# A spectral mixer on one core: the second forward product with real and imaginary halves in one 512-column operand, the row exchange on ScalarE, and a new table of ranks

## The chip, the cores and the metric

The kernel runs on one core of one Trainium2 chip, as one program. The metric is the device time of one execution in microseconds (us), the median of three runs. A core has five engines that work side by side, each through its own queue in order: TensorE (PE, matrix products, with a row of its own, PEld, for the loads of the weights), VectorE (DVE), ScalarE (ACT), GpSimd (POOL, which here issues transfers that add in memory) and SyncE (SP, which issues the other transfers). Matrix products are written to PSUM; other operands lie in SBUF, over 128 partitions.

## The reference

Two branches work on the same input x (2048 rows, 512 columns) and are mixed by a gate per row:

```python
def reference(A_x, A_w_r, A_w_i, B_x, B_w1, B_b1, B_w2, B_b2, gate_w):
    g = sigmoid((x * gate_w).sum(-1, keepdims=True))
    X = rfft2(x, axes=(-2, -1)) * (w_r + 1j * w_i)      # x = A_x
    a = irfft2(X, s=(S, D), axes=(-2, -1))
    b = einsum("bsf,fd->bsd", gelu(einsum("bsd,df->bsf", x, w1) + b1), w2) + b2
    return g * a + (1 - g) * b                           # S, D, F = 2048, 512, 1792
```

Everything is float32. The kernel splits each operand of a product into a high part of 12 bits and a low rest (names ending in h and l), and adds three products: high with high, high with low, low with high.

## The kernel before

**The transform branch.** The 2048 rows are taken as 16 blocks j of 128 rows (row 16a + j of x is row a of block j). `forward(j)` folds a block's 512 columns on VectorE into even and odd parts (tiles `eo`, then `cl`, also shown under the name of the buffer `xr` it reuses), splits them (`eoh`, `eol`) and multiplies by the cosine and sine table `cf` on PE: for c = 0 (real) and c = 1 (imaginary) a product into PSUM tile `pd`, four matmuls of 260 columns and four of 130 per block. ScalarE and VectorE cut `pd` into `x..h` and `x..l`. Then comes the second forward product, a transform over the 128 rows of the block: `py`, with the table `tf` of cosines (64 columns) and sines (64 columns) as weights. Real and imaginary parts need the two halves of `tf` in opposite order, so ScalarE first widens `tf` from 128 to 192 columns (line 710), and each c has three matmuls of 258 columns into a PSUM tile of its own: two high ones (`s_high`) and a low one (`s_low`), six per block. ScalarE copies `py0` to `pys` (line 757), VectorE adds it to `py1` for the real half of `y` (line 758) and subtracts it for the imaginary half, whose two sets of 64 rows change places: on VectorE itself for the first four blocks (line 767), and with a subtraction on VectorE (line 761) and two copies on ScalarE (line 764) for the other twelve. Radix-4 steps over the blocks (`stage1`), the multiplication by the spectral weights (`filt`) and the way back (`stage4`, `inverse`: products `pz` and `pa`) follow.

**The dense branch.** `mlp(half, c)` runs for two halves of F and four groups c of 512 rows: products `ph` (w1; 12 matmuls of 512 columns for each of 7 blocks of F), gelu on ScalarE (line 1106), a split into `g..h` and `g..l`, and products `po` (w2). Partial results go to memory and are added there by POOL's transfers.

**What sets the order.** Each operation is a step of a graph with a cost and an engine; a planner (`Graph.schedule`) plays the engines through and takes, whenever one is free, the ready step of lowest rank whose buffers can be had. The ranks stand in a table of numbers, `RANKS`, one for each step, which replaces the ranks in the code. So the order of every engine's queue, SP's transfers included, comes out of `RANKS`, of the costs (`c_vec`, `c_act`, `c_pe`) and of the numbers of buffers (`slots`, `most`); on the chip each queue then runs in that order, and an operation that waits holds up what stands behind it on its engine. A helper `mm` issues every matmul, so all of PE's rows show one line, 530.

The start: eleven matmuls on zeros warm PE up; then the first `ph` is made in two halves, for two row blocks each (blocks 0 and 4, then 8 and 12), from `mxh` (ScalarE, line 649) and `mxl` (VectorE, line 650), the high part and the rest of x. The end: the last `pa` goes through ScalarE (`od`, line 999) and VectorE (`uv`, `y`, `o`), while PE makes the last `po` in half-width products.

Of the kernel before, what the change touches and what calls it, by code (L numbers as in the profile page):

```python
# [11 lines left out]
F32 = mybir.dt.float32  # L12
# [5 lines left out]
P = 128  # L18
# [154 lines left out]
class Graph:  # L173
# [282 lines left out]
def tile_kernel(ctx: ExitStack, tc: tile.TileContext, xt, w1, w2, b1, b2, x0g, wf, wrev, out, consts):  # L456
# [13 lines left out]
             "so": 2, "ba": 2,  "pf": 2, "pm": 4, "ti": TI, "ring": RING, "hw": 8}  # L470

    whole = ("xr", "xm", "wra", "wrb", "e2", "z", "ttab", "xhl", "wa", "wb", "hid", "so", "ba", "ctab", "gb")
    most = {("pm", "ph"): 2, ("pm", "po"): 2, ("pm", "po0"): 1, ("pm", "py"): 3, ("t2k", "pq"): 2}
    g = Graph(slots, most)
    add = g.add

# [17 lines left out]
    def c_pe(n, k=1):  # L494
        return k * (n / 2400 + 0.0135) + 0.005
# [795 lines left out]
```

## Time and profile before

| what | value |
|---|---|
| median of 3 runs | 372.75 us (372.29 to 372.97) |
| span of the profiled execution, first to last instruction | 370.8 us, granted PE clock 0.999 |
| what the median has beyond the span | 1.95 us |
| PE busy | 365.1 us, 1838 matmuls |
| VectorE busy | 327.5 us, 691 instructions |
| ScalarE busy | 229.6 us, 454 instructions |
| POOL busy | 44.1 us |
| mean transfer rate | 170 GB/s, 62.99 MB |

The page gives no time of its own for the profiled execution beside its span. "Busy" counts time in which an instruction of the engine was under way. PE's matmuls overlap each other, so the time that one adds is read from the step between two starts and not from its own duration. "Idle before" and the bracket behind a row name the time an engine stood still ahead of an instruction and what ended it; a name with q at the end (SPq) is the engine's issuing part. The chain of waits is followed back from the last instruction.

### The profile page before, as it was taken

To read this page: it belongs to the slowest core of one execution; us is meant where nothing else is said; L and a number is where in the kernel's file an instruction comes from. 1 tells how busy PE (TensorE), PEld (TensorE's weight loads), DVE (VectorE), ACT (ScalarE), POOL (GpSimd) and SP (SyncE) were. 2 spreads that over 40 slices of the span, in tenths; PEclk is the share of its full clock that TensorE was granted. 3 is DMA by queue.
4 is the path that set the end of the run, shared out by engine and by line. 5 is a ranking of instruction groups with operands and counts; after the bars stand their busy time and mean duration, and the time that the engine had idled before them with its cause. 6 is when DMAs were issued, how large, how long until landed. Compare 5 with 4: busy or idle time off the path is not lost.

```text
span 370.8 us, 5565 instructions
## 1 busy us (share of the span) xinstructions
PE 365.1 (98%) x1838; PEld 309.9 (84%) x1838; DVE 327.5 (88%) x691; ACT 229.6 (62%) x454; POOL 44.1 (12%) x54
## 2 busy tenths in 40 slices
PE   8999999999999999999999999999999999999995
PEld 6888888888888888888888888888888888888885
DVE  4999999999999789999999999588849696789996
ACT  5776587976678735375367213894697549457830
POOL 0000000000000002021032020001403222221031
PEclk9999999999999999999999999999999999999999
DMA  8962899425954216479289762318968999736268
GB/s 276 389 194 73 257 282 342 147 71 151 289 173 141 77 23 170 142 157 256 72 214 267 225 120 55 57 25 291 209 130 112 211 285 187 130 88 139 88 85 198
DMA packets 50868, 62.99 MB, mean 170 GB/s; under 512 B 4656, under 2 KB 31344, under 8 KB 50064
## 3 DMA queue, kind: packets, MB, share of 16 engines
q1 hardware_dynamic: 43496, 49.54, 41.3%
q0 software_dynamic: 7200, 12.85, 23.1%
q8 instruction: 14, 0.23, 0.2%
q10 hardware_dynamic: 144, 0.26, 0.2%
q14 instruction: 14, 0.11, 0.1%
HBM read 38.64 MB, written 23.73 MB: 168 GB/s over the span
## 4 chain that ended last, share of the span: by engine, by line
PE 95%; DVE 1%; DMA 1%; issue 0%; ACT 0%; SPq 0%; DVEq 0%
PE ph L530 41%; PE po L530 40%; PE pz L530 4%; PE pd L530 4%; PE py L530 3%; PE pa L530 3%; DMA xr<-in_xt 1%; DVE uv L1002 0%; DVE y L1021 0%; SPq L588 0%; DVE y L1024 0%; DVE mxl L650 0%; DVE o L1168 0%; ACT mxh L649 0%; ACT od L999 0%
## 5 line engine op out<-in xcount | busy, mean ns | idle before, releaser
L1106 ACT ACTIVATE ph<-ph,b1t 128x512 f32<-128x512 f32 x56 | 36.9, 659 | 41.5 <-PE ph L530 39.9
L949 ACT ACTIVATE sw<-y,al 64x512 f32<-64x512 f32 x32 | 23.0, 722 | 2.2 <-DVE y L812 1.6
L908 DVE TENSOR_TENSOR m<-y,wf 128x514 f32<-128x514 f32 x32 | 20.8, 689 | 0.2
L956 DVE SCALAR_TENSOR_TENSOR pq<-y,al,sw 128x256 f32<-128x256 f32 x32 | 14.4, 481 | 5.9 <-ACT sw L952 5.5
L521 POOL DMA_DIRECT2D bacc<-o x12 | 10.5, 877 | 73.2 <-ACT o L1155 60.2
L521 POOL DMA_DIRECT2D wa7l<-in_w x1 | 1.0, 1017 | 141.0 <-ACT wa7l L582 141.0
L1155 ACT ACTIVATE o<-po 128x512 f32<-128x512 f32 x12 | 7.1, 595 | 15.9 <-PE po L530 15.8
L1152 ACT ACTIVATE o<-po,b2t 128x512 f32<-128x512 f32 x16 | 10.7, 686 | 7.6 <-PE po L530 7.5
L1002 DVE TENSOR_TENSOR uv<-pa,od 128x512 f32<-128x512 f32 x16 | 10.6, 685 | 3.6 <-ACT od L999 3.5
L764 ACT ACTIVATE y<-pys 64x257 f32<-64x257 f32 x24 | 10.0, 418 | 5.2 <-DVE pys L761 4.8
L530 PE MATMUL pd<-cf,eoh 128*128 128x260 f32 x64 | 12.7, 285 | 0.0
L688 DVE TENSOR_TENSOR eo<-xr 128x256 f32<-128x256 f32 x30 | 12.0, 418 | 0.0
L530 PEld LDWEIGHTS pd<-cf,eoh 128*128 128x128 f32 x64 | 10.6, 189 | 1.5 <-issue 0.2
L999 ACT ACTIVATE od<-pa 128x512 f32<-128x512 f32 x8 | 4.8, 599 | 10.2 <-PE pa L530 9.9
L952 ACT ACTIVATE sw<-y 1x512 f32<-1x512 f32 x16 | 10.1, 629 | 0.4
L530 PE MATMUL pd<-cf,eol 128*128 128x130 f32 x64 | 10.3, 253 | 0.0
L702 DVE TENSOR_TENSOR xr<-eo 128x256 f32<-128x256 f32 x24 | 9.8, 418 | 0.1
L530 PEld LDWEIGHTS pd<-cf,eol 128*128 128x128 f32 x64 | 9.6, 189 | 0.1
L649 ACT ACTIVATE mxh<-xm 128x512 fp32r<-128x512 f32 x12 | 6.9, 623 | 3.7 <-PE ph L530 3.7
L650 DVE TENSOR_TENSOR mxl<-xm,mxh 128x512 fp32r<-128x512 f32 x12 | 7.8, 686 | 1.2 <-ACT mxh L649 1.2
L705 DVE TENSOR_TENSOR eol<-xr,eoh 128x512 fp32r<-128x512 f32 x12 | 8.3, 688 | 0.2
L1046 DVE SCALAR_TENSOR_TENSOR ba<-gb,ba 128x512 f32<-128x512 f32 x12 | 8.1, 685 | 0.3 <-DMA ba<-bacc 0.3
(713 smaller groups left out, 1353.6 us busy)
## 6 DMA issues: line engine op xcount, KB each, us to landing
wf<-in_wf SPq DMA_DIRECT2D x16, 257.0 KB, 4.9
bacc<-o SPq DMA_DIRECT2D x16, 256.0 KB, 3.3
xr<-in_xt SPq DMA_DIRECT2D x15, 256.0 KB, 3.5
war<-in_w SPq DMA_DIRECT2D x14, 256.0 KB, 3.5
wbr<-in_w SPq DMA_DIRECT2D x14, 256.0 KB, 3.5
xm<-in_xt SPq DMA_DIRECT2D x12, 256.0 KB, 4.3
bacc<-o POOLq DMA_DIRECT2D x12, 256.0 KB, 4.0
ba<-bacc SPq DMA_DIRECT2D x12, 256.0 KB, 3.2
```

The lines of the kernel that those rows point to most:

```text
L521: return add("pool", kb / 150, 3.4, lambda: nc.gpsimd.dma_start(dst(), src(), accum_op=ALU.add), reads, writes, rank)
L530: pe.matmul(ps, w, x, start=start, stop=stop)
L688: v(lambda s=s, op=op: vec.tensor_tensor(eo.ap()[:, s], x.ap()[:, 0:2], x.ap()[:, 2:4], op=op), 256, [x], [(eo, s)], FEED)
L702: v(lambda k=k, op=op: vec.tensor_tensor(quarter(cl, k), eo.ap()[:, :, 0], eo.ap()[:, :, 1], op=op), 256, [eo], [(cl, k)] if j % 4 == 0 or ...
L764: a(lambda o=o, i=i: act.activation(Y[j].ap()[o:o + HP, 1], pys.ap()[i:i + HP, 1], AF.Copy), 257, [(pys, 1)], [(Y[j], 1 + k)], 0, more=0.1)
L908: v(lambda mk=mk, k=k, y=y, w=w: vec.tensor_tensor(mk.ap(), y.ap(), w.ap()[:, k:k + 1, :ND].to_broadcast([P, 2, ND]), op=ALU.mult), 514, [ ...
L949: a(lambda sw=sw, y=y, o=o, i=i: act.activation(sw.ap()[o:o + HP], y.ap()[i:i + HP, ::-1, :HD], AF.Copy, scale=al.ap()[i:i + HP, 0:1]), 51 ...
L952: a(lambda sw=sw, y=y, j=j: act.activation(sw.ap()[HP:HP + 1], y.ap()[HP:HP + 1, ::-1, :HD], AF.Copy, scale=math.cos(math.pi * j / NJ)), 5 ...
L956: v(lambda sw=sw, pq_=pq_, y=y, j=j, k=k, op=op: vec.scalar_tensor_tensor(pq_.ap()[:, k], y.ap()[:, k, :HD], al.ap()[:, 1 + j:2 + j], sw.a ...
L1002: v(lambda i=i, op=op: vec.tensor_tensor(uv.ap()[:, :, i], ps.ap()[:, 0], od.ap(), op=op), 512, [ps, od], [(uv, i)], 2)
L1106: a(lambda f=f, ps=ps: act.activation(ps.ap(), ps.ap(), AF.Gelu_apprx_tanh, bias=b1t.ap()[:, f:f + 1]), 600, [b1t], [ps], 0.9 if half else ...
L1152: a(lambda o=o, ps=ps, q=q: act.activation(o.ap(), ps.ap(), AF.Identity, scale=-1.0, bias=b2t.ap()[:, q:q + 1]), 600, [b2t, ps], [o])
```

## The change

In `forward(j)` the cut of `pd` keeps 128 columns from each of its two parts instead of 129, so that `x..h` and `x..l` hold the real and the imaginary half side by side in 2 x 256 = 512 columns. The second forward product then has `tf` as it is loaded (128 columns, not widened) as weights and all 512 columns as moving operand: two high matmuls and one low one per block, into one PSUM tile `py`. The imaginary half comes out with its two sets of 64 rows in the wrong places; ScalarE exchanges them in two copies of 64 rows out of PSUM into one of two buffers `sh` (used in turn, with a column of zeros in the middle, written once by two small memsets). VectorE's addition and subtraction then read `py` and `sh`, over 256 columns; the last of the 257 columns of `y` is made by two one-column copies on ScalarE.

```diff
-    most = {..., ("pm", "py"): 3, ...}
+    most = {..., ("pm", "py"): 2, ...}
     def c_pe(n, k=1):
-        return k * (n / 2400 + 0.0135) + 0.005
+        return k * max(n / 2400 + 0.0135, 0.112)
...
+    sh = [one(f"sh{k}", [P, ND], parts=3) for k in range(2)]
+    for b in sh:
+        add("vec", 0.1, 0.1, lambda b=b: vec.memset(b.ap()[:, P:P + 1], 0.0), [], [(b, 2)], 0.7)
...
-        t = buf("ttab", [P, 2, P + HP], F32R, f"tf{j}", parts=2)
-        dma(lambda: raw(t.ap()[:, :, :P], tf_d[j]), 128, [], [(t, 0)])
-        a(lambda: act.activation(t.ap()[:, :, P:], t.ap()[:, :, :HP], AF.Copy), P, [(t, 0)], [(t, 1)])
+        t = buf("ttab", [P, 2, P], F32R, f"tf{j}")
+        dma(lambda: raw(t.ap(), tf_d[j]), 128, [], [t])
...
-            return some(c, [[511, 2], [1, P + 1]], 1 + k * NC)
+            return some(c, [[510 + c, 2], [1, P]], 2 + k * NC)
...
-        py = [buf("pm", [P, 512], F32, f"py{j}{c}", pool=pp, cls="py") for c in range(2)]
-        pys = t2k(f"pys{j}", cls="pys", parts=2)
+        py = buf("pm", [P, 2, HD], F32, f"py{j}", pool=pp, cls="py")
+        b = sh[NORD.index(j) % 2]
...
-        def s_high(c):
+        def s_high():
             for k in range(2):
-                mm(py[c].ap()[:, :NE], ttab(k, c), xh.ap()[:, c, :NE], k == 0, False)
-        def s_low(c):
-            mm(py[c].ap()[:, :NE], ttab(0, c), xl.ap()[:, c, :NE], False, True)
-        for c in range(2):
-            m(lambda c=c: s_high(c), NE, 2, [t, (xh, c)], [py[c]], 0)
-        for c in range(2):
-            m(lambda c=c: s_low(c), NE, 1, [t, (xl, c)], [py[c]], 0)
-        a(lambda: act.activation(pys.ap()[:, 0], py[0].ap()[:, 1:NE], AF.Copy), 257, [py[0]], [(pys, 0)], 0)
-        v(lambda: vec.tensor_tensor(Y[j].ap()[:, 0], py[1].ap()[:, 1:NE], pys.ap()[:, 0], op=ALU.add), 257, [py[1], (pys, 0)], [(Y[j], 0)], 0)
+                mm(flat(py), t.ap()[:, k], flat(xh), k == 0, False)
+        m(s_high, 512, 2, [t, xh], [py], 0)
+        m(lambda: mm(flat(py), t.ap()[:, 0], flat(xl), False, True), 512, 1, [t, xl], [py], 0)
         halves = ((0, HP), (HP, 0))
+        for k, (o, i) in enumerate(halves):
+            a(lambda o=o, i=i: act.activation(around(b.ap()[o:o + HP]), py.ap()[i:i + HP, 1].rearrange("p (a b) -> p a b", a=2), AF.Copy), HD,
+              [py], [(b, k)], 0)
+        v(lambda: vec.tensor_tensor(Y[j].ap()[:, 0, :HD], py.ap()[:, 0], b.ap()[:, :HD], op=ALU.add), HD, [py, b], [(Y[j], 0)], 0)
+        a(lambda: act.activation(Y[j].ap()[:, 0, HD:], b.ap()[:, HD:], AF.Copy), 1, [(b, 0), (b, 1)], [(Y[j], 0)], 0)
+        a(lambda: act.activation(Y[j].ap()[:, 1, HD:], py.ap()[:, 1, HD - 1:], AF.Copy), 1, [py], [(Y[j], 1), (Y[j], 2)], 0)
...
-    -149, 43, 217, 3, 143, 100, 150, 574, 1118, 447, 437, 885, 624, 1856, 1001, 866, 832, 912, 1753, 1799, 1869, 396,
```

The whole table `RANKS` is new as well (its first line of before is shown), and with it the order of all queues. The planner's cost of a matmul has a floor of 0.112 us and no longer a share per step. What the new order does at three places, with the tiles' numbers:

PE, around the second forward product of block 0 (`py00` and `py01` before, `py0` now; `po` and `g` belong to the dense branch). Before:

```order
L530 MATMUL py00_440<-x0h_421,tf0_112 128x258 x2
L530 MATMUL po0_010_254<-g0_2h_272,wb2h_311 128x512
...
L530 MATMUL pd40_455<-cf_132,eoh4_339 128x260 x2
L530 MATMUL py00_440<-x0l_426,tf0_112 128x258
L530 MATMUL pd41_461<-cf_132,eoh4_339 128x260 x2
L530 MATMUL pd40_455<-cf_132,eol4_434 128x130 x2
...
L530 MATMUL py01_477<-x0h_421,tf0_112 128x258 x2
L530 MATMUL pd41_461<-cf_132,eol4_434 128x130 x2
L530 MATMUL py01_477<-x0l_426,tf0_112 128x258
```

Now:

```order
L531 MATMUL py0_444<-x0h_432,tf0_126 128x512 x2
L531 MATMUL po0_010_257<-g0_3h_334,wb3h_338 128x512
L531 MATMUL po0_010_257<-g0_3l_340,wb3h_338 128x512
L531 MATMUL po0_010_257<-g0_3h_334,wb3l_344 128x512
L531 MATMUL py0_444<-x0l_435,tf0_126 128x512
L531 MATMUL pd40_458<-cf_110,eoh4_376 128x260 x2
L531 MATMUL pd40_458<-cf_110,eol4_380 128x130 x2
L531 MATMUL pd41_468<-cf_110,eoh4_376 128x260 x2
L531 MATMUL pd41_468<-cf_110,eol4_380 128x130 x2
```

Six matmuls of 258 columns have become three of 512; the products `pd` of the next block, which stood among them, now follow them.

VectorE, at the start (`xr4`, `xr8`, `xr12` are x of blocks 4, 8 and 12; `mxl` is the rest after the high part `mxh`; `gq` is a small operation for the gate). Before:

```order
L650 TENSOR_TENSOR mxl00_125<-xf0_76,mxh00_110 128x4x128
L650 TENSOR_TENSOR mxl00_125<-xr4_82,mxh00_110 128x4x128
L620 TENSOR_TENSOR gq_144<-gs_114 128x2
L650 TENSOR_TENSOR mxl00_125<-xr12_98,mxh00_110 128x4x128
L650 TENSOR_TENSOR mxl00_125<-xr8_96,mxh00_110 128x4x128
L577 TENSOR_TENSOR wa1l_160<-war1_100,wa1h_140 128x512
```

Now:

```order
L655 TENSOR_TENSOR mxl00_128<-xf0_76,mxh00_114 128x4x128
L655 TENSOR_TENSOR mxl00_128<-xr4_100,mxh00_114 128x4x128
L655 TENSOR_TENSOR mxl00_128<-xr8_102,mxh00_114 128x4x128
L655 TENSOR_TENSOR mxl00_128<-xr12_104,mxh00_114 128x4x128
L578 TENSOR_TENSOR wa1l_162<-war1_106,wa1h_147 128x512
```

Block 8 now comes ahead of block 12, as ScalarE makes their high parts (and made them before); the gate's operation has moved behind the weights.

SP, the first transfers (`war` are blocks of w1, `wbr` of w2, `b1t` the bias of the first dense product). Before:

```order
L1064 DMA war0_78<-in_w1 128x512
L588 DMA xr4_82<-in_xt 128x512
L588 DMA xr8_96<-in_xt 128x512
L588 DMA xr12_98<-in_xt 128x512
L1064 DMA war1_100<-in_w1 128x512
L1064 DMA wbr0_102<-in_w2 128x512
L634 DMA b1t_104<-in_b1 128x14
```

Now:

```order
L1071 DMA war0_78<-in_w1 128x512
L639 DMA b1t_86<-in_b1 128x14
L589 DMA xr4_100<-in_xt 128x512
L589 DMA xr8_102<-in_xt 128x512
L589 DMA xr12_104<-in_xt 128x512
L1071 DMA war1_106<-in_w1 128x512
```

The load of `b1t` has moved from the seventh place to the second, ahead of the three loads of x.

More of the change, by code (lines that the diff above doesn't have):

```diff
@@ L472, in tile_kernel @@
     whole = ("xr", "xm", "wra", "wrb", "e2", "z", "ttab", "xhl", "wa", "wb", "hid", "so", "ba", "ctab", "gb")
-    most = {("pm", "ph"): 2, ("pm", "po"): 2, ("pm", "po0"): 1, ("pm", "py"): 3, ("t2k", "pq"): 2}
+    most = {("pm", "ph"): 2, ("pm", "po"): 2, ("pm", "po0"): 1, ("pm", "py"): 2, ("t2k", "pq"): 2}
     g = Graph(slots, most)
@@ L724, in body @@
         def body(c, k):
-            return some(c, [[511, 2], [1, P + 1]], 1 + k * NC)
+            return some(c, [[510 + c, 2], [1, P]], 2 + k * NC)
         def two(t, c):
-            return t.ap()[:, c, :NE].rearrange("p (a b) -> p a b", a=2)
-        xh = buf("z", [P, 2, 512], F32R, f"x{j}h", parts=2)
-        xl = buf("z", [P, 2, 512], F32R, f"x{j}l", parts=2)
+            return t.ap()[:, c].rearrange("p (a b) -> p a b", a=2)
+        xh = buf("z", [P, 2, HD], F32R, f"x{j}h", parts=2)
+        xl = buf("z", [P, 2, HD], F32R, f"x{j}l", parts=2)
         n = j % 4 * 4 + j // 4
@@ L736, in forward @@
         for c in range(2):
-            a(lambda c=c: act.activation(two(xh, c), body(c, 0), AF.Copy), 258, [pd[c]], [(xh, c)], 0)
-            v(lambda c=c: vec.tensor_tensor(two(xl, c), body(c, 0), two(xh, c), op=ALU.subtract), 258, [pd[c], (xh, c)], [(xl, c)], 0)
-            v(lambda c=c: vec.tensor_tensor(two(xl, c), two(xl, c), body(c, 1), op=ALU.add), 258, [pd[c]], [(xl, c)], 0)
+            a(lambda c=c: act.activation(two(xh, c), body(c, 0), AF.Copy), HD, [pd[c]], [(xh, c)], 0)
+            v(lambda c=c: vec.tensor_tensor(two(xl, c), body(c, 0), two(xh, c), op=ALU.subtract), HD, [pd[c], (xh, c)], [(xl, c)], 0)
@@ L740, in forward @@
+            v(lambda c=c: vec.tensor_tensor(two(xl, c), two(xl, c), body(c, 1), op=ALU.add), HD, [pd[c]], [(xl, c)], 0)
             a(lambda c=c: act.activation(logit.ap()[:, n, c], some(c, [[641, 2], [NC, 2]], 0), AF.Copy), 4, [pd[c]],
               [(logit, 2 * n + c)], 0)
-        py = [buf("pm", [P, 512], F32, f"py{j}{c}", pool=pp, cls="py") for c in range(2)]
-        pys = t2k(f"pys{j}", cls="pys", parts=2)
-        def s_high(c):
-            for k in range(2):
-                mm(py[c].ap()[:, :NE], ttab(k, c), xh.ap()[:, c, :NE], k == 0, False)
@@ new lines, in around @@
+        def around(x):
+            return bass.AP(tensor=x.tensor, offset=x.offset, ap=[list(x.ap[0]), [P + 1, 2], [1, P]])
+        for k, (o, i) in enumerate(halves):
[3 more added lines that the diff above has]
+        a(lambda: act.activation(Y[j].ap()[:, 0, HD:], b.ap()[:, HD:], AF.Copy), 1, [(b, 0), (b, 1)], [(Y[j], 0)], 0)
@@ L760, in forward @@
+        a(lambda: act.activation(Y[j].ap()[:, 1, HD:], py.ap()[:, 1, HD - 1:], AF.Copy), 1, [py], [(Y[j], 1), (Y[j], 2)], 0)
         if j in BY_ACT:
-            v(lambda: vec.tensor_tensor(pys.ap()[:, 1], py[1].ap()[:, 1:NE], pys.ap()[:, 0], op=ALU.subtract), 257, [py[1], (pys, 0)],
-              [(pys, 1)], 0)
+            pys = buf("t2k", [P, HD], F32, f"pys{j}", cls="pys")
+            v(lambda: vec.tensor_tensor(pys.ap(), b.ap()[:, :HD], py.ap()[:, 0], op=ALU.subtract), HD, [py, b], [pys], 0)
@@ L763, in forward @@
             for k, (o, i) in enumerate(halves):
-                a(lambda o=o, i=i: act.activation(Y[j].ap()[o:o + HP, 1], pys.ap()[i:i + HP, 1], AF.Copy), 257, [(pys, 1)], [(Y[j], 1 + k)], 0, more=0.1)
+                a(lambda o=o, i=i: act.activation(Y[j].ap()[o:o + HP, 1, :HD], pys.ap()[i:i + HP], AF.Copy), HD, [pys], [(Y[j], 1 + k)], 0, more=0.1)
         else:
@@ L767, in forward @@
                 add("vec", 0.45, 0.1, lambda o=o, i=i: vec.tensor_tensor(
-                    Y[j].ap()[o:o + HP, 1], py[1].ap()[i:i + HP, 1:NE], pys.ap()[i:i + HP, 0], op=ALU.subtract),
-                    [(pys, 0), py[1]], [(Y[j], 1 + k)], 0)
+                    Y[j].ap()[o:o + HP, 1, :HD], b.ap()[i:i + HP, :HD], py.ap()[i:i + HP, 0], op=ALU.subtract),
+                    [b, py], [(Y[j], 1 + k)], 0)
         if j // 4 == 3:
@@ L897, in filt @@
             y = ys[q1]
-            w = buf("xr", [P, 2, 288], F32, f"wf{k2}")
+            w = buf("xr", [P, 2, 272], F32, f"wf{k2}")
             dma(lambda w=w, k2=k2: sp.dma_start(w.ap()[:, :, :ND], wf[k2]), 257, [], [w], 3)
```

4 lines of the change are left out of this document (2 added, 2 removed), and 218 rows, old and new, of the table RANKS.

## The prediction

> **What bounds the kernel now.** I read the page's busy times and chain first, then stretches of the span, then single pieces of the chain and the first and last ten microseconds.
>
> ```profile
> span 370.8 us, 5565 instructions
> PE 365.1 (98%) x1838; PEld 309.9 (84%) x1838; DVE 327.5 (88%) x691; ACT 229.6 (62%) x454; POOL 44.1 (12%) x54
> ...
> PE 95%; DVE 1%; DMA 1%; issue 0%; ACT 0%; SPq 0%; DVEq 0%
> PE ph L530 41%; PE po L530 40%; PE pz L530 4%; PE pd L530 4%; PE py L530 3%; PE pa L530 3%; DMA xr<-in_xt 1%; DVE uv L1002 0%; DVE y L1021 0%; SPq L588 0%; DVE y L1024 0%; DVE mxl L650 0%; DVE o L1168 0%; ACT mxh L649 0%; ACT od L999 0%
> ```
>
> TensorE is busy 98% of the span and 95% of the chain that ended last; its products py, which the change rewrites, are 3% of it. A busy PE need not be a full one, so I look for holes.
>
> ```profile
> core 0: us, PE busy (x) PEld busy (x) DVE busy (x) ACT busy (x) POOL busy (x), PEclk, DMA share, GB/s
> ...
> 30.00:118.00 88.00, 88.00 (x489) 76.22 (x488) 85.47 (x203) 62.81 (x169) 0.00 (x0) 1.00 0.65 200
> 118.00:140.00 22.00, 22.00 (x99) 18.16 (x99) 18.55 (x37) 13.37 (x24) 0.00 (x0) 1.00 0.17 47
> 140.00:230.00 90.00, 90.00 (x399) 74.53 (x398) 86.92 (x181) 42.97 (x71) 14.99 (x17) 1.00 0.68 173
> 230.00:240.00 10.00, 10.00 (x46) 8.29 (x45) 5.70 (x10) 7.87 (x12) 0.87 (x1) 1.00 0.24 36
> ```
>
> The forward transform is the stretch 30 to 118. PE has no hole there; VectorE is at 97% (85.47 of 88), ScalarE at 71%. So only two things can move the end: PE's own time for its products, and what stands before its first and after its last matmul. The clock is full (1.00), so no change comes from there.
>
> **PE: the products py.** What one matmul takes is read from the steps between starts, since the durations overlap.
>
> ```profile
> 114.84 1.08 PE py L530 x9
> ...
> 141.40 2.72 PE ph L530 x12
> ```
> ```profile
> 98.26 0.64 PE py L530 x5
> ```
>
> Nine matmuls of 258 columns in 1.08 us are 0.120 us each; twelve of 512 columns in 2.72 us are 0.2267 us each. Each of the 16 blocks had six of 258 (two high and one low product, for real and imaginary part) and now has three of 512. That is 96 x 0.120 = 11.52 us before and 48 x 0.2267 = 10.88 us after: 0.64 us less. The columns hardly change (24,768 against 24,576); what goes is a fixed share: the two rows give (226.7 - 120) / 254 = 0.42 ns a column and 11.6 ns a matmul, and 48 matmuls fewer are 0.56 us. The upper bound is from the dearer row, 0.64 for five: 96 x 0.128 = 12.3, so 1.4 us less. I stay near the lower one and take 0.74 us, because the dear ones follow 130-column matmuls:
>
> ```profile
> 35.78 0.34 PE L530 MATMUL pd<-cf,eol 128*128 128x130 f32 x2
> 35.96 0.33 PE L530 MATMUL py<-x4l,tf 128*128 128x258 f32 x1
> 36.13 0.40 PE L530 MATMUL pd<-cf,eoh 128*128 128x260 f32 x2
> 36.37 0.33 PE L530 MATMUL pd<-cf,eol 128*128 128x130 f32 x2
> 36.54 0.45 PE L530 MATMUL po<-g_4h,wb4h 128*128 128x512 f32 x1
> 36.82 0.40 PE L530 MATMUL po<-g_4l,wb4h 128*128 128x512 f32 x1
> ```
>
> After a pair of 130 the 258-column py takes 0.17 instead of 0.12, and the 512-column po 0.28 instead of 0.23: the same 0.05 either way, so whatever follows such a pair pays it. There are 32 such pairs before and after; the 0.05 moves to another product and isn't saved.
>
> The Trainium skill (TensorE: Matmul & The Clock Gate, Back-to-back issue gap) speaks against this term: it gives N / 2.4 + 2.5 ns for an isolated step at full clock. By that the estimate is 96 x 110 = 10.56 against 48 x 215.8 = 10.36, a saving of 0.20 us and not 0.74. The rows here, 120 and 226.7, disagree with it at both widths, and by the same 10 to 11 ns.
>
> **The start.** Here the new order changes something on the path.
>
> ```profile
> 1.20 1.36 SPq L588 DMA_DIRECT2D xr<-in_xt  x3
> ...
> 3.55 0.44 SPq L634 DMA_DIRECT2D b1t<-in_b  x1
> 4.31 0.43 DVE L574 CAST wa0h<-war 128x512 fp32r<-128x512 f32 x1 [3.31 <-DMA war<-in_w]
> ...
> 5.01 1.29 ACT L649 ACTIVATE mxh<-xr 128x512 fp32r<-128x512 f32 x2
> ...
> 6.60 0.15 DVE L620 TENSOR_TENSOR gq<-gs 128x2 f32<-128x2 f32 x1
> ...
> 6.89 0.63 ACT L649 ACTIVATE mxh<-xr 128x512 fp32r<-128x512 f32 x1 [0.58 <-DMA xr<-in_xt]
> ...
> 7.55 1.29 DVE L650 TENSOR_TENSOR mxl<-xr,mxh 128x512 fp32r<-128x512 f32 x2 [0.80 <-ACT mxh L649]
> 7.57 0.53 PEld L530 LDWEIGHTS ph<-mxh,wa0h 128*128 128x128 f32 x4 [0.30 <-ACT mxh L649]
> ...
> 8.15 0.63 PE L530 MATMUL ph<-mxh,wa0l 128*128 128x256 f32 x4
> ...
> 8.90 0.54 PEld L530 LDWEIGHTS ph<-mxl,wa0h 128*128 128x128 f32 x4 [0.32 <-DVE mxl L650]
> ```
>
> The third xr (block 12) lands last, at 6.89. VectorE's queue holds block 12's difference ahead of block 8's, whose input has been ready since ScalarE ended its second operation at 5.01 + 1.29 = 6.30; so both are made after 7.55 and PE waits 0.32 us at 8.90. In the new order block 8's difference is first, and runs in VectorE's 0.80 us of idle time; block 12's ends near 7.55 + 0.69 = 8.24, before the four matmuls from 8.15 have started (8.15 + 4 x 0.12 = 8.63). PE then saves 8.90 - 8.63 = 0.27 us. What is late next there is the landing itself, and that the change may delay: the load of b1t now stands second in SP's queue, ahead of the three xr, and its issue took 0.44 us. If the landing slips by all of it, PE loses 0.44 - 0.27 = 0.17 us; if the transfers themselves set it, nothing slips. xr's third issue ended at 1.20 + 1.36 = 2.56 and its data were there at 6.89, 4.3 us later, where the page's median for such a load is 3.5:
>
> ```profile
> xr<-in_xt SPq DMA_DIRECT2D x15, 256.0 KB, 3.5
> ```
>
> So most of a microsecond was spent behind other transfers, and I take a slip of 0.10. The start gives 0.27 - 0.10 = 0.17 us, between a gain of 0.27 and a loss of 0.17.
>
> **ScalarE and VectorE.** Per block ScalarE gains two exchanges of 64 x 256 and two one-column copies and loses the 128x257 copy of py and the widening of tf.
>
> ```profile
> L764 ACT ACTIVATE y<-pys 64x257 f32<-64x257 f32 x24 | 10.0, 418 | 5.2 <-DVE pys L761 4.8
> L757 ACT ACTIVATE pys<-py 128x257 f32<-128x257 f32 x16 | 6.2, 385 | 2.9 <-PE py L530 2.8
> L740 ACT ACTIVATE logit<-pd 128x4 f32<-128x4 f32 x32 | 5.4, 177 | 4.1 <-PE pd L530 3.7 <-DVE x13l L738 0.2 <-DVE x1l L738 0.2
> L710 ACT ACTIVATE tf<-tf 128x128 fp32r<-128x128 f32 x16 | 4.9, 316 | 1.4 <-DMA tf<-tf 1.3
> ```
>
> No row exchanges halves out of PSUM; the nearest are L764 (exchange, out of SBUF) and L757 (out of PSUM, no exchange). With the dearer: 2 x 0.418 + 2 x 0.177 - 0.385 - 0.316 = 0.49 us a block, 7.8 us in all; with the cheaper 6.8 us. ScalarE then has 62.8 + 7.8 = 70.6 of 88 us: it fits, so nothing on the path. VectorE keeps its additions and subtractions (256 columns for 257) and gets two one-column memsets; the gq row above, the nearest in size, took 0.15, and VectorE idles 3.31 us up to 4.31 in any case. If that cover went, the memsets would cost 0.3 us at most. VectorE's y now waits for two ScalarE operations in a row where it waited for one, about 0.4 us later; it costs nothing as long as VectorE has other work in front of it, as it had before:
>
> ```profile
> who waited for it (us, times):
> ...
>   DVE y L758: 0.2, 1
> ```
>
> The new py takes one PSUM buffer where the pair took two, which can only ease PE.
>
> **The end.**
>
> ```profile
> 361.33 0.40 PE L530 MATMUL pa<-z11l,ci 128*128 128x256 f32 x2
> ...
> 361.77 0.60 ACT L999 ACTIVATE od<-pa 128x512 f32<-128x512 f32 x1 [4.01 <-PE pa L530]
> ...
> 366.13 0.28 PE L530 MATMUL po<-g_13h,wb13l 128*128 128x256 f32 x1
> 366.13 0.75 DVE L1168 SCALAR_TENSOR_TENSOR o<-gb,po 128x256 f32<-128x256 f32 x2
> ```
>
> From the last pa VectorE's chain and PE's last 39 half-width products end together near 366.1. The new order has 39 such products there too, and the same VectorE and SP rows behind them, so I take nothing.
>
> **Sum.** The profiled execution's span is 370.8 us; the median of the runs is 372.75, so 1.95 us lie around the span, and I leave those. 0.74 + 0.17 = 0.91 us less, 372.75 - 0.91 = 371.84, given as 371.8 us. Everything between start and end that the new order shuffles I cost at nothing, as PE showed no hole there.
>
> **The rivals.** *The fixed share isn't saved* (372.5 us). For it: the change shortens no column stream, only 192 columns x 0.42 ns = 0.08 us, and the new order could set more alternations between 130-column pairs and long products; 0.66 us of gain are gone after 13 more stalls of 0.05. Against it: the two steps above are steady over nine and twelve matmuls. 372.75 - 0.08 - 0.17 = 372.5. The skill's estimate above would put the time at 372.75 - 0.20 - 0.17 = 372.4, on the same side.
>
> *VectorE stands behind the exchange* (374.0 us, slower). The exchange lies between PE's py and VectorE's y, in two queues that keep their order; behind y stand the differences xl that PE's next low product needs. At 0.42 us in each of 16 blocks VectorE loses 6.7 us in a stretch where it has 88 - 85.47 = 2.53 us idle; 4.2 us are pushed out, and if half of that reaches PE it is 2.1 us: 372.75 - 0.91 + 2.1 = 373.9, about 374.0. It decides once VectorE's waits for the exchange pass 2.5 us. Against it: only 0.2 us of such a wait before.
>
> *More is saved* (371.1 us): the dear row of 0.128 is the rule, and b1t delays nothing: 372.75 - 1.4 - 0.27 = 371.1.
>
> **How the numbers follow.** The forecast gets 0.52, the fixed share not saved 0.23, slower 0.12, more saved 0.13. The likeliest's own range is 371.3 to 372.4. About 0.2%, 0.75 us, is what a measurement of this kernel can tell from no change: below 372.0 is faster, above 373.5 slower. Two thirds of the forecast (0.35), all of the larger gain (0.13) and a tenth of the second case (0.02) lie below 372.0: 0.50. Slower is 0.12, and 0.38 is left for no change. The range 371.0 to 373.2 leaves out the slower case and a part of the larger gain.
>
> **What would show it.** In the changed profile: py as 48 matmuls at steps of 0.227 us, PE's total for them near 10.9 us; PE's wait before the low half of ph_0 gone, and the third xr landing between 6.9 and 7.4; ScalarE 7 to 8 us busier and VectorE as before; no wait of VectorE for sh above a few tenths in all; last matmul near 365.2. I am wrong in the first term if steps of py come out above 0.235 us, in the second if the third xr lands after 7.2, and altogether if PE shows waits between 10 and 360 us.

## The result, and the profile after it

The changed kernel took 377.21 us in the median against 372.52 us of the kernel before on the same chip, a ratio of 1.0126 (95% interval 1.0112 to 1.014): slower, where 371.8 us had been forecast. A second set of runs on another chip gave 376.33 against 373.19 us, 1.0092 (1.0056 to 1.0127). One execution of the first set, the one that was profiled, ran its matmuls at half the rate from end to end (738.97 us, 512 columns in 0.44 us, for a cause that stays open) and is left out of these medians and ratios, as are two of h3_honest_vec at 379.05 and 379.94 us. The profile read here is therefore one of the second set, which took 375.86 us.

The page of the changed kernel: its span, the engines' busy times, and the chain by engine and by line.

```profile
span 374.0 us, 5497 instructions
PE 366.8 (98%) x1790; PEld 306.2 (82%) x1790; DVE 327.1 (87%) x693; ACT 236.0 (63%) x486; POOL 44.1 (12%) x54
...
PE 88%; ACT 5%; DVE 3%; DMA 1%; issue 1%; SPq 0%; DVEq 0%
PE ph L531 38%; PE po L531 37%; PE pz L531 4%; PE pd L531 3%; PE pa L531 3%; PE py L531 2%; ACT sh L762 1%; DMA xf<-in_x0g 1%; ACT y L771 1%; DMA rev<-in_wrev 0%; ACT o L1159 0%; DVE o L1175 0%; DVE y L1028 0%; ACT L1205 0%; ACT L1202 0%
```

PE is as busy in its share as it was, but its part of the chain fell from 95% to 88%. ScalarE, which had 0% of it, holds 5%, and the exchange (line 762) and the shifted copy of the difference (line 771) stand in it by name.

Where the time goes is read from three stretches, first of the kernel before, then of the changed one. The columns after the stretch are PE, PEld, DVE, ACT and POOL, each with its busy time and its instructions in brackets.

```profile
0.00:30.00 30.00, 28.65 (x130) 23.50 (x131) 24.70 (x59) 20.34 (x39) 0.20 (x4) 1.00 0.78 269
30.00:130.00 100.00, 100.00 (x543) 86.11 (x542) 95.29 (x224) 72.55 (x185) 0.00 (x0) 1.00 0.60 185
130.00:420.00 290.00, 236.41 (x1169) 200.26 (x1167) 207.56 (x409) 136.73 (x231) 43.88 (x50) 1.00 0.54 126
```
```profile
0.00:30.00 30.00, 28.57 (x132) 23.54 (x133) 25.39 (x62) 19.78 (x36) 0.20 (x4) 1.00 0.78 269
30.00:130.00 100.00, 98.81 (x480) 80.14 (x479) 92.40 (x214) 77.48 (x213) 0.00 (x0) 1.00 0.61 183
130.00:420.00 290.00, 239.46 (x1181) 202.55 (x1179) 209.33 (x418) 138.73 (x238) 43.94 (x50) 0.99 0.56 126
```

Count PE's matmuls. In the first 30 us the changed kernel is two ahead. Between 30 and 130 us it has 48 fewer to do for the same work (three instead of six in each of 16 blocks), 543 - 48 = 495, and does 480. Fifteen short at 0.227 us are 3.4 us, and the spans differ by 374.0 - 370.8 = 3.2 us. After 130 us it has 12 more left and never gets them back. So the whole loss is in the forward part. "PE busy" shows only 1.2 us of it (98.81 of 100): matmuls overlap, so one that starts late while the one before is still ending leaves less idle time than it loses. Two neighbouring rows show it:

```profile
70.84 0.39 PE L531 MATMUL ph<-mxh,wa3l 128*128 128x512 f32 x1
71.47 0.73 PE L531 MATMUL py<-x2h,tf 128*128 128x512 f32 x2 [0.24 <-ACT x2h L738]
```

The py starts 0.63 us after the ph, where such a step takes 0.227. It is 0.40 us late, and the bracket says 0.24. Added up over all of PE's steps between 30 and 130 us, against 0.227 us for 512 columns, 0.120 for 258 and 260 and 0.109 for 130, the starts are 5.0 us late, in the kernel before 1.1. The 4.0 us between the two, less 0.64 for the shorter py, are the 3.4 us again. PE's listed waits are short, as the bracket was; two of those that the kernel before had not:

```profile
PE pd L531 <- DVE x2l L740: 0.3, 1, 0.3
PE ph L531 <- DVE g_1l L578: 0.3, 1, 0.3
```

The wait for x2l, followed back along the chain (start, length, what; other pieces of it left out):

```profile
63.23 0.17 ACT y L766
...
63.41 0.38 ACT sh L762
...
63.80 0.38 ACT sh L762
...
64.21 0.39 ACT x13h L738
...
67.11 0.60 ACT g_1h L577
...
67.73 0.41 ACT y L771
...
68.16 0.42 ACT y L771
...
68.58 0.38 ACT sh L762
...
68.98 0.38 ACT sh L762
...
69.39 0.39 ACT x2h L738
...
71.91 0.43 DVE x2l L740
...
72.48 0.54 PE pd L531 x3
```

A one-column copy waits for PE's last py of a block; behind it two exchange copies, splits and a gelu, the two shifted copies of the difference and the next block's two exchange copies stand in ScalarE's one queue, which also waits 0.81 us for VectorE's x13l on the way. Only then comes x2h, the split that VectorE's x2l and PE's next product need. (The piece between x2h and x2l is VectorE's; its wait there is shown with the first experiment.)

### The profile page after: what moved, and what is told of

It is laid out like the page before. It is cut to its first block, busy times and chain, and to the rows that moved or that the text cites. A ratio compares the mean times of both kernels' runs of the same rounds, so it can differ in the third digit from the quotient of the medians.

```text
span 737.1 us, 5497 instructions
## 1 busy us (share of the span) xinstructions
PE 732.2 (99%) x1790; PEld 505.1 (69%) x1790; DVE 332.3 (45%) x693; ACT 239.2 (32%) x486; POOL 44.3 (6%) x54
## 4 chain that ended last, share of the span: by engine, by line
PE 99%; DVE 0%; DVEq 0%; issue 0%
PE ph L531 43%; PE po L531 43%; PE pz L531 4%; PE pd L531 3%; PE py L531 3%; PE pa L531 3%; PE none L531 1%; PE pown L531 0%; DVE o L1175 0%; DVE o L1180 0%; DVEq L1290 0%; DVE zero L598 0%; DVE sh L595 0%
## 5 line engine op out<-in xcount | busy, mean ns | idle before, releaser
L531 PEld LDWEIGHTS pd<-cf,eoh 128*128 128x128 f32 x64 | 17.9, 300 | 7.1 <-issue 6.3
L531 PE MATMUL pd<-cf,eoh 128*128 128x260 f32 x64 | 20.9, 458 | 0.0
L578 DVE TENSOR_TENSOR g_7l<-ph,g_7h 128x512 fp32r<-128x512 f32 x4 | 2.8, 690 | 37.6 <-ACT g_7h L577 37.6
L531 PEld LDWEIGHTS pd<-cf,eol 128*128 128x128 f32 x64 | 17.9, 338 | 1.3 <-issue 1.0
L762 ACT ACTIVATE sh<-py 64x256 f32<-64x256 f32 x32 | 12.2, 380 | 15.0 <-PE py L531 14.4
L531 PE MATMUL pd<-cf,eol 128*128 128x130 f32 x64 | 15.3, 354 | 0.0
L769 DVE TENSOR_TENSOR pys<-sh,py 128x256 f32<-128x256 f32 x12 | 5.0, 418 | 15.7 <-ACT sh L762 9.1
L531 PE MATMUL po<-g_7h,wb7l 128*128 128x512 f32 (+1 forms) x17 | 11.5, 675 | 0.0
L531 PE MATMUL po<-g_9l,wb9h 128*128 128x512 f32 (+1 forms) x17 | 11.4, 670 | 0.0
L531 PE MATMUL po<-g_8h,wb8h 128*128 128x512 f32 (+1 forms) x17 | 11.4, 668 | 0.0
```

Source lines behind the costliest of these rows:

```text
L531: pe.matmul(ps, w, x, start=start, stop=stop)
L762: a(lambda o=o, i=i: act.activation(around(b.ap()[o:o + HP]), py.ap()[i:i + HP, 1].rearrange("p (a b) -> p a b", a=2), AF.Copy), HD, [py], ...
```

## The experiments

Three theories were tested against each other. **S**: the exchange is dearer than the order was planned for, so ScalarE's queue runs late in the forward part. **O**: the new order itself is at fault. **C**: the one-column copies hold ScalarE's queue while they wait for PE. "Matmuls" is PE's count between 30 and 130 us in the windows of each run's profile; 495 would be no loss against the kernel before. A profile is of one execution, which can lie about 1 us off the median given with it.

**The changed kernel again, nothing edited.**

> The changed kernel as it is, for a profile at its usual time (about 377.5 us), since its profiled execution took 739 us with every matmul at half speed (512 columns in steps of 0.43 us). Theory 1, late full speed: TensorE runs its first matmuls at 0.43 us a step of 512 for some 10 us longer than before (where the clock was granted at 4.84 us), which costs half of that, 5 us; from then on steps are 0.2267 and there are no holes; py takes 10.9 us in all. Theory 2, VectorE stands behind the row exchange: full speed comes at about 5 us as before, and PE shows waits of about 5 us in sum between 30 and 120 us, while VectorE waits over 2.5 us for sh. Theory 3, the long operand itself is dearer: steps of py come out at 0.30 us and over, which gives 48 x 0.08 = 3.8 us.

Measured: 376.33 us, 480 matmuls. Full speed was not late: the four half-width products that start at 6.33 us take 0.48 us, 0.12 each. And the matmuls of 512 columns are not dear: two py take 59.93 - 59.47 = 0.46 us here, 0.23 each. The first and the third theory fall.

```profile
59.47 0.62 PE L531 MATMUL py<-x9h,tf 128*128 128x512 f32 x2
59.93 0.39 PE L531 MATMUL ph<-mxh,wa1h 128*128 128x512 f32 x1
```

The second, VectorE behind the exchange, holds only in part. PE's listed waits between 25 and 125 us come to 1.1 us and not to 5 (the rest shows as late starts alone), and VectorE waits 1.0 us for sh, not over 2.5. VectorE's own list of waits in the same stretch:

```profile
DVE y L764 <- ACT y L766: 1.5, 4, 0.6
DVE pys L769 <- ACT sh L762: 1.0, 2, 0.6
...
DVE pys L769 <- ACT y L766: 0.5, 1, 0.5
```

That is 3.0 us for ScalarE's copies of py, two thirds of it behind the one-column copy L766 and not behind the exchange itself. One such place, VectorE's two rows and ScalarE's row between them:

```profile
69.39 0.42 DVE L769 TENSOR_TENSOR pys<-sh,py 128x256 f32<-128x256 f32 x1 [0.37 <-ACT sh L762]
70.05 0.42 DVE L764 TENSOR_TENSOR y<-py,sh 128x256 f32<-128x256 f32 x1 [0.24 <-ACT y L766]
```
```profile
69.85 0.17 ACT L766 ACTIVATE y<-py 128x1 f32<-128x1 f32 x1
```

The exchange had ended at 69.36 (68.98 + 0.38 in the chain above). The addition y still starts at 70.05, when the one-column copy is done, and that copy started when the subtraction pys was done (69.81). The two write different columns of y; what they share is py, which both read. In this program two engines that read one accumulator take turns in the planned order, so each read that is added on ScalarE is a hand-over to VectorE and back.

**One copy for the two exchange copies**, the planned order kept and the exchange of rows left out (the four runs from here to the old order were made side by side):

```diff
-            a(lambda o=o, i=i: act.activation(around(b.ap()[o:o + HP]), py.ap()[i:i + HP, 1]..., AF.Copy), HD,
+            a(lambda k=k: k or act.activation(around(b.ap()), py.ap()[:, 1]..., AF.Copy), HD,
```

> The changed kernel in its own order, with the two 64-row exchange copies of each of the 16 blocks replaced by one copy of all 128 rows that does not exchange them (the row exchange is left out, so the values are not the reference's). Theory S, ScalarE's queue runs late because an exchange pair takes about 0.93 us there against 0.56 us in the planner's price: one 128x256 copy takes about 0.39 us with a step near 0.27, ScalarE gets some 10 us back, PE's time lost between 30 and 130 us falls from about 7 to about 3 us, and the time is 372 us or less, ratio to the kernel before 0.990 to 1.000. Rival O, the new order itself (TensorE's order meets its operands too late whatever the exchange costs): the time stays at 375.5 us or more, ratio above 1.006. Rival C, the one-column copies hold ScalarE's queue behind TensorE: little change too, above 375.

Measured: 374.01 us against 372.66, ratio 1.0037 (1.0009 to 1.0064), 490 matmuls, where the changed kernel had 1.0092 and 1.0126. O and C fall as sole causes, since both wanted 375 us or more. S is right in direction, but 2 us of its gain are missing. The cost of the exchange on the chip comes out here. Two pieces of ScalarE's queue, of the changed kernel and of this one:

```profile
67.73 0.84 ACT L771 ACTIVATE y<-pys 64x256 f32<-64x256 f32 x2
68.58 0.78 ACT L762 ACTIVATE sh<-py 64x256 f32<-64x256 f32 x2
69.39 0.39 ACT L738 ACTIVATE x2h<-pd 128x256 fp32r<-128x256 f32 x1
```
```profile
67.34 0.84 ACT L771 ACTIVATE y<-pys 64x256 f32<-64x256 f32 x2
68.08 0.37 ACT L762 ACTIVATE sh<-py 128x256 f32<-128x256 f32 x1
68.48 0.38 ACT L738 ACTIVATE x2h<-pd 128x256 fp32r<-128x256 f32 x1
```

From the first row to x2h it is 1.66 us with the exchange and 1.14 without. The planner had the two copies at 0.28 us each.

**No one-column copies**, planned order kept (the last column is left out and set to zero once, by VectorE):

```diff
-        a(lambda: act.activation(Y[j].ap()[:, 0, HD:], b.ap()[:, HD:], AF.Copy), 1, ...)
-        a(lambda: act.activation(Y[j].ap()[:, 1, HD:], py.ap()[:, 1, HD - 1:], AF.Copy), 1, ...)
+        a(lambda: None, 1, ...)
+        a(lambda: None, 1, ...)
...
```

> The changed kernel in its own order without the 32 one-column copies on ScalarE (the last column of the transformed blocks is left out and set to zero once, so the values are not the reference's). Rival C, the one-column copies hold the in-order queue of ScalarE behind the last matmul of each block (2.2 us of waits stand at one of the two lines): 2 us or more are gained, the time is 374.5 us or less. Theory S: each of them is 0.05 to 0.18 us long, 16 x about 0.2 us of 236 us, and the exchanges are still there: at most 1.2 us are gained, the time stays at 375 us or more. Rival O: no change, 376 to 377.5 us.

Measured: 374.19 us, 1.0039 (1.0018 to 1.0061), 491 matmuls. That is what C expected and more than S allowed. Half of these copies are the hand-overs seen above. The 32 copies of 0.17 to 0.2 us give back as much here, about 2 us, as 16 exchange copies of 0.4 us did; that it is the hand-overs among them that weigh is likely but was not tried apart.

**The two copies unshifted**, each writing the rows it reads (the exchange left out again):

```diff
-            a(lambda o=o, i=i: act.activation(around(b.ap()[o:o + HP]), py.ap()[i:i + HP, 1]..., AF.Copy), HD,
+            a(lambda o=o, i=i: act.activation(around(b.ap()[o:o + HP]), py.ap()[o:o + HP, 1]..., AF.Copy), HD,
```

> The changed kernel in its own order; the two 64-row copies of each block stay, but each writes the rows that it reads (the exchange of the halves is left out, so the values are not the reference's). If the shift from one half of the partitions to the other is what keeps these copies from overlapping their neighbours: their start-to-start step falls from 0.40 us to about 0.27 us, ScalarE gets 0.13 x 32 = 4 us back and the time falls by 1.5 us or more, to 375 us or less. If a copy of 64 rows alone does it: the step stays at 0.39 to 0.41 us and the time at 376 to 377.5 us. Rivals O and C expect no change of the time in either case.

Measured: 375.8 us, 1.0068 (1.0046 to 1.0091), 485 matmuls: between the two answers, and not told apart from the changed kernel's second set (1.0056 to 1.0127). The rows say why so little came of it.

```profile
37.59 0.63 ACT L709 ACTIVATE eoh<-xr 128x512 fp32r<-128x512 f32 x1
38.13 0.75 ACT L762 ACTIVATE sh<-py 64x256 f32<-64x256 f32 x2
38.90 0.66 ACT L738 ACTIVATE x8h<-pd 128x256 fp32r<-128x256 f32 x2
...
43.47 0.37 ACT L738 ACTIVATE x12h<-pd 128x256 fp32r<-128x256 f32 x1
43.86 0.77 ACT L762 ACTIVATE sh<-py 64x256 f32<-64x256 f32 x2
44.53 0.16 ACT L741 ACTIVATE logit<-pd 128x4 f32<-128x4 f32 x1
```

At 38.13 the pair starts 0.09 us before eoh has ended, and x8h starts 0.02 us after the pair; at 43.86 it is the other way round. In the queue of the first case the copy of rows 0 to 63 stands first, in the second the copy of rows 64 to 127. So neither the shift nor the count of 64 rows does it: two ScalarE instructions that begin at the same row overlap by some 0.1 us, and where the half changes they don't. With the real exchange input and output change halves at every step, and the pair loses the overlap three times, on the way in, between the two, and on the way out. The Trainium skill (ScalarE: Activation LUTs, What ACT_TABLE_LOAD costs) has back-to-back instructions overlap by about 93 ns; the rows here agree for one half and show no overlap across halves.

**The old order's ranks on the new product** (the ranks of the kernel before carried over to the changed steps, the planner's old price of a matmul):

```diff
-        return k * max(n / 2400 + 0.0135, 0.112)
+        return k * (n / 2400 + 0.0135) + 0.005
...
```

> The change's product and row exchange, complete, but with the order numbers of the kernel before carried over to the changed steps and TensorE's old price in the planner. Rival O, the new order is at fault: this runs at 372.5 us or less, ratio 1.000 or under. Theory S, the exchange is dear wherever it stands on ScalarE: slower than the kernel before by 1.5 us or more, 374 to 378 us, with PE's lost time in the forward part again above 5 us.

Measured: 379.55 us, 1.0179 (1.0164 to 1.0194), 471 matmuls. O's short form, that an order near the old one repairs the change, falls. The time lies above what S expected too (374 to 378 us); some 3.7 us of it belong to one long stall and a fall of the clock behind it (last section).

**Both cuts at once** (with the next two, side by side on another chip):

```diff
+            a(lambda k=k: k or act.activation(around(b.ap()), py.ap()[:, 1]..., AF.Copy), HD,
...
+        a(lambda: None, 1, ...)
+        a(lambda: None, 1, ...)
...
```

> The changed kernel in its own order with both cuts: one unexchanged 128-row copy for the two exchange copies of each block, and no one-column copies (the row exchange and the last column are left out, so the values are not the reference's). Each cut alone gave some 2.5 to 3 us. If both work through the one thing, ScalarE's queue that runs late in the forward part, the second cut adds less than the first, but what is left of TensorE's waits goes too: TensorE's lost time between 30 and 130 us is 2 to 3 us as in the kernel before, and the time falls to 371 to 372.5 us, ratio 0.995 to 1.000, which is what the product's shorter stream and the earlier start are worth. If something besides ScalarE holds the new order up (VectorE's order, a transfer), it stays at 373 us or more.

Measured: 373.74 us, 1.0027 (1.0008 to 1.0046), 493 matmuls. The two cuts don't add up, as expected of one queue, and PE's late starts fall from 5.0 to 2.0 us (1.1 in the kernel before). The time does not reach 372.5, so something besides these copies is left.

**The kernel before with more work for ScalarE:**

```diff
-        a(lambda: act.activation(pys.ap()[:, 0], py[0].ap()[:, 1:NE], AF.Copy), 257, ...)
+        a(lambda: [act.activation(pys.ap()[:, 0], py[0].ap()[:, 1:NE], AF.Copy) for _ in range(3)], 257, ...)
```

> The kernel before, in its own order, with its 128x257 copy of py (one in each of the 16 blocks) made three times over, so that ScalarE has 32 more copies of about 0.27 us step, 8.6 us in all, about what the change adds to that engine (its output stays the reference's). Theory S, a later ScalarE queue in the forward part costs TensorE time by itself: the time rises by 1.5 to 5 us, to 374.2 to 377.5 us, with the loss between 30 and 130 us. Rival: ScalarE has room there (it is busy 62.8 of 88 us), and the change's loss comes from its order or its operands: the time stays within 0.7 us of 372.7.

Measured: 381.29 us against 372.89, 1.022 (1.0191 to 1.0248), 505 matmuls where the kernel before does 543. Of the 8.6 us put in, 8.4 came out at the end; S had the sign, and at most 5 us of the size. Who waits for the copy:

```profile
DVE pys L761 <- ACT pys L757: 2.5, 3, 0.9
...
PE ph L530 <- ACT pys L757: 2.0, 4, 1.3
PE py L530 <- ACT pys L757: 1.8, 3, 1.0
```

PE waits for the accumulator that the copy has still to empty. ScalarE, busy 62.8 of 88 us in the kernel before, had no room at this place. It is not the same wait as in the changed kernel, where PE's listed waits are for splits: the run shows how little slack there was, and not the path of the change's loss.

**The one-column copies on GpSimd:**

```diff
+        a(lambda: nc.gpsimd.tensor_copy(Y[j].ap()[:, 0, HD:], b.ap()[:, HD:]), 1, ...)
+        a(lambda: [nc.gpsimd.tensor_copy(Y[j].ap()[o:o + HP, 1, HD:], b.ap()[i:i + HP, HD:]) for o, i in halves], 1, ...)
```

> The changed kernel in its own order, complete, with the 32 one-column copies issued on GpSimd (16 of 128x1 and 32 of 64x1, all from sh) in place of ScalarE. Theory C (the one-column copies stand in ScalarE's queue): like the kernel without them, 373 to 375 us. If GpSimd is slow to free sh, or holds VectorE up, 376 us or more.

Measured: 415.97 us, 1.1152. Its copies take 0.18 to 0.20 us each, 9.3 us in all, and the kernel is some 39 us slower than the changed one. By the two profiles 27 us of that are PE standing idle (34.1 of 414.9 us against 7.2 of 374.0), and 14 us are PE at work for longer (380.8 against 366.8) at a granted clock of 0.953; why PE has to wait was not settled. C is not answered by it.

**Prices from the traces, and a new search of the order** (the one-column copies at 0.12 us, a new table of ranks; with the next two, side by side on another chip):

```diff
-              [py], [(b, k)], 0)
+              [py], [(b, k)], 0, more=(0.24, 0.12)[k])
...
-        ..., HD, [pys], [(Y[j], 1 + k)], 0, more=0.1)
+        ..., HD, [pys], [(Y[j], 1 + k)], 0, more=(0.22, 0.1)[k])
...
```

> The change, complete, with the order planned anew after the planner's prices were set to what the traces show: 0.52 and 0.40 us for the two exchange copies (0.28 each in the change), 0.55 and 0.43 us for the two copies of L771, 0.12 us for a one-column copy; the ranks were searched again from the change's own planned order, with some lateness of ScalarE, VectorE and the transfers allowed for. Theory S, the order was planned on a ScalarE that is faster than the real one: TensorE's lost time between 30 and 130 us falls from about 7 to 2 to 4 us and the time is 371 to 373 us, 3.5 us or more under the change and within 1.5 us of the kernel before. If the exchange is simply too much for ScalarE whatever the order: 374.5 us or more.

Measured: 374.27 us against 372.5, 1.0047 (1.0034 to 1.0061), 492 matmuls, between the two answers: half of the change's loss or more is gone, in a complete kernel whose ScalarE is as busy as the changed one's (236.0 us). Prices and search changed together here.

**The same, one-column copies on VectorE:**

```diff
+        add("vec", 0.08, 0.12, lambda: vec.tensor_copy(Y[j].ap()[:, 0, HD:], b.ap()[:, HD:]), ...)
+        add("vec", 0.08, 0.12, lambda: vec.tensor_copy(Y[j].ap()[:, 1, HD:], py.ap()[:, 1, HD - 1:]), ...)
...
```

> As the one before (complete, prices from the traces, ranks searched again), with the 32 one-column copies on VectorE in place of ScalarE. Theory S: ScalarE is eased further, VectorE pays 32 x about 0.07 us; 370.5 to 372.5 us. If VectorE, which is busy 82.3 of 88 us in the forward part, can't take them: 373.5 us or more.

Measured: 373.41 us, 1.0032 (1.0008 to 1.0057), 494 matmuls; the hoped-for 370.5 to 372.5 us are missed, and it is not told apart from the one before.

**The control: the kernel before, ranks searched again** (only RANKS differ).

> The kernel before with its ranks searched again in the same way for as long, prices as they were: the control for the two others. If what they gain came from the search alone, this gains as much against the kernel before (1 us or more, 371.7 us or less); if it comes from the product with honest prices, this stays within 0.7 us of 372.7.

Measured: 375.74 us, 1.0089 (1.0072 to 1.0107), 536 matmuls for 543. The search alone gains nothing; it loses 3.2 us. So an order that is best on the planner's prices is not best on the chip, and O comes back in another form: the table of the kernel before is better than what a fresh plan finds. Against this control the change is ahead by 1.5 us, though with prices of its own; the next searches turn that round. What the fresh orders run into is a transfer; from the chains of h1_honest and of this control:

```profile
48.69 3.76 DMA bacc<-o
```
```profile
46.01 7.05 DMA tf<-tf
```

Behind the first, PE's next wait for a split is 0.9 us long, and behind the second PE waits 0.8 us for tf itself. The first search had allowed for some lateness; the next three take landings up to 1.3 us later than planned into it (only RANKS differ from h1_honest, h3_honest_vec and the kernel before).

> The change, complete, prices of ScalarE's copies from the traces as in h1_honest, ranks searched further with transfers taken to land up to 1.3 us later than the planner's lag. If what was left of the loss in h1_honest (1.8 us against the kernel before, with TensorE standing still at 54.9 us behind a transfer) comes from transfers that land late in the crowded stretch from 46 to 56 us: 1 to 2 us less than h1_honest, 372.3 to 373.3 us. If not: 374 us or more.

Measured: 373.31 us against 372.81, 1.0011 (0.9995 to 1.0026), 496 matmuls: no difference to the kernel before can be told.

```profile
30.00:130.00 100.00, 99.84 (x496) 83.71 (x495) 94.16 (x219) 80.24 (x217) 0.00 (x0) 1.00 0.59 183
```

> As h4_late_transfers, with the one-column copies on VectorE (as h3_honest_vec, which took 373.6 us and varied from 372.7 to 377.2): 371.5 to 373 us and less spread if late transfers were what was left, 373.5 us or more if not.

Measured: 373.64 us, 1.0029 (1.0013 to 1.0046), 492 matmuls. No gain over h3_honest_vec: a miss.

> The kernel before, ranks searched again in the same way, with late transfers allowed for: the control. The first search without them made it 3.2 us slower (375.7 us), with TensorE waiting for a transfer of tf; if allowing for late transfers is what helps, it comes back to 372 to 373.5 us. If a searched order loses on the chip for another reason, it stays at 375 us or more.

Measured: 372.63 us, 0.9999 (0.9984 to 1.0015), 543 matmuls: the control recovers all of its 3.2 us. That fits late transfers as what its first search lacked, as far as one more searched table can show it. The change (373.31 us) is not ahead of this control.

## Why the prediction was wrong

The change costs 3.4 to 4.7 us. With ScalarE's new work cut down in the same order (f3_both) the ratio falls from 1.0092 or 1.0126 to 1.0027, so most of the loss in that order hangs on this work. The work alone does not make it, since complete kernels with all of it came nearer. With the copies' prices from the traces and a new search 1.7 to 2.9 us were gone (1.0047), and about 1.3 us more with a search that allows for later landings (1.0011; with the one-column copies on VectorE that second search gained nothing). How much of this is the prices and how much the searching stays open: no run has the changed kernel searched anew at its old prices. No version beat the kernel before.

- **The term that failed: "Everything between start and end that the new order shuffles I cost at nothing, as PE showed no hole there."** It measured 4.0 us of late starts between 30 and 130 us, more than all the gains forecast. No hole means that the old order just kept PE fed. It says nothing of the slack behind it, and the load test showed, at the copy of py, that there was none.
- **"ScalarE then has 70.6 of 88 us: it fits, so nothing on the path" failed too.** The busy time was forecast well, 6.8 to 7.8 us more against 236.0 - 229.6 = 6.4. But room in the average is not room in the queue: in the chain shown above x2h stands behind the copies, and PE behind x2h.
- **The shorter product stream (0.74 us)** is right in its steps, 0.23 us each. In h4_late_transfers, where PE hardly waits, the starts between 30 and 130 us are 1.5 us late against 1.1 before, which eats most of the 0.64. So the term reaches the end in no measured time: h4_late_transfers and the control hc_before_late_transfers can't be told apart.
- **The start (0.17 us)** came out larger. The third landing was not delayed by b1t (6.50 us, 6.89 before), and the wait before the low half of ph_0 is gone:

```profile
6.50 0.63 ACT L654 ACTIVATE mxh<-xr 128x512 fp32r<-128x512 f32 x1 [0.15 <-DMA xr<-in_xt]
...
8.73 0.40 PE L531 MATMUL ph<-mxh,wa1h 128*128 128x512 f32 x1
```

  PE's first full-width ph starts at 8.73 us, where it was 9.48, a gain of 0.75 instead of 0.17. Part of that is luck: in the five other kernels with this same table of ranks it stood between 8.64 and 9.41, last where PE's first four half-width products, here 0.58 us, took 1.02 (f8_unshifted).
- **The end (0)** held: from the end of PE's last matmul to the end of the span it is 4.5 us, where it was 4.4.
- **The slower rival, VectorE behind the exchange (374.0 us, 0.12)**, came nearest. VectorE's waits for ScalarE's copies of py came to 3.0 us, over the 2.5 named, but only 1.0 of them for the exchange; the rest was for the one-column copies, which it did not count. Its price was too low by 2.3 to 3.2 us. It counted only VectorE's queue, and by the chain ScalarE's own splits came late behind the same copies. The argument against it, only 0.2 us of such a wait before, was none, because the operations waited for were new.
- **The sign it named was right:** "altogether if PE shows waits between 10 and 360 us". It did, in short waits and longer late starts.
- **The Trainium skill's spacing (TensorE: Matmul & The Clock Gate, Back-to-back issue gap)**, N / 2.4 + 2.5 ns, gives 215.8 ns for 512 columns. The rows after the change have 0.23 us as those before had; the formula that would have cut the saving to 0.20 us is not borne out.

## What to carry to other kernels

When a queue that runs in order gains work, ask not how busy its engine is but what stands behind the new instruction in that queue and who waits for it: repeat an existing copy twice and measure, and the slack at that place is known. An order that a planner makes holds only as far as its prices; a new kind of instruction needs its price measured between its real neighbours before the order is made, and a short one that waits for another engine can cost its wait and not its length. Compare a newly planned order with the old kernel planned anew by the same means, or the order's loss is taken for the change's.

## What the runs showed that was not expected

**ScalarE: changing the half of the rows costs the overlap**, about 0.12 us a change (from some 0.1 us before the end of the instruction ahead to 0.01 to 0.02 us after it), as the rows of the unshifted copies show.

**PE: behind a stall of 2.1 us the clock was halved for 3.4 us.** In the run with the old order's ranks:

```profile
125.79 0.39 PE L532 MATMUL po<-g_1h,wb1l 128*128 128x512 f32 x1
128.25 0.50 PE L532 MATMUL ph<-mxh,wa4h 128*128 128x512 f32 x1 [2.08 <-DVE g_2l L579]
...
128.82 0.63 PE L532 MATMUL ph<-mxh,wa4l 128*128 128x512 f32 x1
129.25 0.63 PE L532 MATMUL ph<-mxh,wa4h 128*128 128x512 f32 x1
...
132.23 0.40 PE L532 MATMUL ph<-mxl,wa4h 128*128 128x512 f32 x1
```

The steps are 0.43 us from 128.82 to 132.23 instead of 0.227, eight of them, 1.6 us more on top of the stall, and the granted clock reads 0.60 between 128 and 132 us. The longest wait of PE in the control hc_before_late_transfers, 1.2 us, had no such effect. In g4_pool_columns steps of 0.43 us follow stalls of 2.58 us and of 2.75 us:

```profile
245.40 0.50 PE L531 MATMUL ph<-mxl,wa7h 128*128 128x512 f32 x1 [2.75 <-DMA mxl<-xs0l]
```

They also follow three shorter stalls within 5 us there (1.57, 0.59 and 0.91, up to 59.33 us), so the length of a single stall is not the whole condition. The Trainium skill (TensorE: Matmul & The Clock Gate, What's actually happening) puts the fall after an idle window of about 3.4 us; here 2.1 us were enough.

**GpSimd as a place for 48 tiny copies made the kernel some 39 us slower** than it was with 32 on ScalarE, with copies of 0.2 us.
